# Local and global attention in front of a mixture of experts: the values as the stationary operand, in 64x64 parts, with the biases added on TensorE

## The chip, the cores and the metric

One core of a Trainium2 chip runs the kernel. The metric is the device time of one execution in microseconds. TensorE is called PE here (its weight loads have a row of their own, PEld), VectorE is DVE, ScalarE is ACT, GpSimd is POOL, and SyncE is SP, which issues most of the DMAs. Each of these engines takes its instructions in the order in which the program has them; they wait for each other through semaphores.

## The reference

Attention with a causal window of 96 keys and 8 global keys, with a bias that grows with the distance, in fp32; its output goes through a top-2 mixture of 8 experts.

```
q, k, v: [4, 8, 768, 64]
scores = q k^T / 8 + bias;  bias = -slope[h] * dist
keep   = (key < 8) | (0 <= query - key < 96)
a      = exp(scores - rowmax) / (rowsum + 1e-9)
x      = (a v), heads side by side: [3072, 512]
logits = x w_gate;  noisy = logits + log1p(exp(x w_noise)) * noise
out[token] = sum over the token's 2 best experts of weight * relu(x w1[e]) w2[e]
```

## The kernel before

Three stages follow each other: attention with the gate (tokens in 24 blocks of 128, six to a batch row), then the first expert, whose tokens are collected by gathers from a table in DRAM, then the other experts. The change touches the first stage and the gate, which is spread over it. In the expert stage only the order of the rows of w1 changes, on the host.

The unit of attention is `n`, one of 96: a block `g` of 128 queries and a pair index `u` of four. It covers two heads, which lie on the lower and the upper 64 partitions, for the two halves `s` of 64 queries. The first block of each batch row (i = 0) has 128 keys, every other block has 168 for each half (96 before, 8 global, 64 own). For each `n`:

- `product` (L485), issued for two `n` at a time: q in 64x64 parts is stationary and the keys are streamed, four parts of the array at once. The scores land in one bank of PSUM per `n`, out of a ring of three.
- `score` (L497, L501): for each half, one DVE instruction adds the bias, scales and takes the row's maximum, and one ACT instruction takes the exponential from SBUF.
- `trans` (L513, L515): PE transposes the probabilities, four parts of 128x128 for two halves and two ranges of keys, into a PSUM bank of the ring `at`, and one ACT copy of up to 512 columns brings them to SBUF.
- `attend` (L533): the transposed probabilities are the stationary operand, 128 columns each, and the values are streamed, 65 columns a head. The 65th column is all ones and gives the row's sum. DVE divides (L539 to L542) and has the block's output rows `xr`.

The gate of block `g` follows a few `n` later: `gate_t` transposes `xr` (L192) and ACT copies it (L194), `gate_l` multiplies by the gate's weights (L200) and ACT copies (L203), `gate_s` sums partial results (L206) and leaves the logits in a PSUM bank of their own. `gate_t` also issues the store of `xr` to DRAM. `route` is a generator that makes the top-2 choice and the table for a segment of blocks. Each call of `tick` takes one small step of it, nearly all on DVE.

The order is written out by hand: one loop over `n` calls `trans(n)`, `score(n+2)`, `attend(n-2)` and, for every other `n`, `product(n+3)`; a table `todo` puts loads, gates and the splitting of weights at chosen `n`. The PSUM rings matter below: `at` and `m` (transposes and the gate) share banks 3 and 4 in turn, so every tile taken from them waits until the tile before the last one has been read. At the end of the loop `turn` (L171) transposes the first expert's gathered tokens.

Of the kernel before, what the change touches and what calls it, by code (L numbers as in the profile page):

```python
# [20 lines left out]
P = 128  # L21
NP = 96
# [8 lines left out]
def tile_local_global_attention_then_moe(  # L31
# [3 lines left out]
    kT: bass.AP,  # L35
    v: bass.AP,
# [14 lines left out]
    D1 = D + 1  # L51
    E, _, F = w1.shape
    KC, FC = Dm // P, F // P
    NG = kT.shape[2] // NB - P
# [3 lines left out]
    WIN = NP + NG + Q  # L58
    windowed = 1 <= n_local <= NP + 1 and 0 <= n_global <= NG
# [16 lines left out]
    rings = {"sc": [0, 1, 2], "at": [3, 4], "m": [3, 4], "av": [5, 6], "lg": [7]}  # L76
    turns = {}
# [15 lines left out]
    sel = consts.tile([P, 2 * E], F32, name="sel")  # L93
# [89 lines left out]
    XR, XT, LS = {}, {}, {}  # L183
    lg = bank("lg")
    lgv = lg[:, :NT * 2 * E].rearrange("p (t e) -> p t e", t=NT)

    def gate_t(g):
        x = XR.pop(g).rearrange("p h d -> p (h d)")
        nc.sync.dma_start(xd[DUMP + g * P:DUMP + (g + 1) * P], x)
        ps = bank("m").rearrange("p (k t) -> p k t", k=KC)  # L190
        for k in range(KC):
            nc.tensor.transpose(ps[:, k], x[:, k * P:(k + 1) * P], ident)  # L192
        XT[g] = gp.tile([P, KC, P], F32, name="xt")
        nc.scalar.activation(XT[g], ps, AF.Copy)  # L194

    def gate_l(g):
        ps = bank("m")[:, :P]
        x = XT.pop(g)
        for k in range(KC):
            nc.tensor.matmul(ps[32 * k:32 * k + 32], wgn[:, k], x[:, k], start=True, stop=True,  # L200
                             tile_position=(0, 32 * k))
        LS[g] = gp.tile([P, P], F32, name="ls")
        nc.scalar.activation(LS[g], ps, AF.Copy)  # L203

    def gate_s(g):
        nc.tensor.matmul(lgv[:, g], LS.pop(g), sel, start=True, stop=True)  # L206
# [4 lines left out]
    def route(r):  # L211
# [4 lines left out]
        l = small.tile([P, SW, 2 * E], F32, name=f"l{r % 2}")[:, :w]  # L216
        u, t, p, ny, po = (small.tile([P, SW, E], F32, name=f"{x}{r % 2}")[:, :w] for x in ("u", "t", "p", "ny", "po"))
        n = l[:, :, E:]
        nc.vector.tensor_copy(l, lgv[:, a:z])
        yield  # L220
# [54 lines left out]
        ps = lg[:, NT * 2 * E:]  # L275
# [47 lines left out]
    with ExitStack() as actx:  # L323
# [6 lines left out]
        KB = NG + P  # L330

        def load_qk(b, j, i0):

            if i0 == 0:
                qs[b, j] = qbuf[j]
                ks[b, j] = aw.tile([P, KC, NP + NBH * KB], F32, name="ks")
            a = i0 * KB - (NP if j and not i0 else 0)
            c0 = j * NBH * KB
            nc.sync.dma_start(ks[b, j][:, :, NP + a:NP + (i0 + 1) * KB],
                              kT[b, :, c0 + a:c0 + (i0 + 1) * KB].rearrange("(k p) t -> p k t", p=P))  # L340
# [4 lines left out]
        HD = H * D1  # L345

        def load_v(g):

            b, i = divmod(g, NB)
            vs[g] = aw.tile([P, HD], F32, name="vs", bufs=4)  # L350
            nc.sync.dma_start(vs[g], v[b, i])
            if i:
                vp[g] = vpb[g % 4]
                nc.sync.dma_start(vp[g][:NP], v[b, i - 1, P - NP:])
                if i <= 4:
                    nc.sync.dma_start(vp[g][NP:], v[b, 0, :NG])

        if windowed:
            vpb = [ac.tile([NP + NG, HD], F32, name=f"vp{j}") for j in range(4)]
# [3 lines left out]
            load_qk(0, 0, 1)  # L363
            load_v(1)
            load_qk(0, 0, 2)
# [3 lines left out]
            bias0 = ac.tile([P, KC, 2, P], F32, name="bias0")  # L369
            bias = ac.tile([P, KC, 2, WIN], F32, name="bias")  # L370
            dist0 = ac.tile([Q, 2, P], F32, name="dist0")
            dist = ac.tile([Q, 2, WIN], F32, name="dist")
            far = 1e9 / min(slopes)

            def iota(d, base, step=0):

                nc.gpsimd.iota(d, pattern=[[step, d.shape[1]], [-1, d.shape[2]]], base=base, channel_multiplier=1,
                               allow_small_or_imprecise_dtypes=True)

            def reach(d, base, step, fill):  # L380

                n, w = d.shape[1:]
                if base < w:
                    nc.gpsimd.affine_select(out=d, in_=d, pattern=[[step, n], [-1, w]], compare_op=OP.is_ge,
                                            fill=fill, base=base, channel_multiplier=1)
                nc.gpsimd.affine_select(out=d, in_=d, pattern=[[-step, n], [1, w]], compare_op=OP.is_ge, fill=fill,
                                        base=n_local - 1 - base, channel_multiplier=-1)

            def biases(to, d, heads):
                for h in heads:  # L390
                    u, y = h // 4 * 2 + h % 2, h // 2 % 2
                    nc.vector.tensor_scalar(to[y * Q:(y + 1) * Q, u], d, -slopes[h] / scale, None, op0=OP.mult)
# [4 lines left out]
            iota(dist0, 0, Q)  # L397
            if n_global:
                reach(dist0[:, :, :n_global], 0, Q, float(n_local))
            reach(dist0[:, :, n_global:], -n_global, Q, far)  # L400
            make_identity(nc, ident)
            for x in range(2):
                c = NP - x * Q
                d = dist[:, x:x + 1]
                for a, z, base in (0, c, NP), (c + NG, WIN, x * Q):
                    iota(d[:, :, a:z], base)
                    reach(d[:, :, a:z], base, 0, far)
                nc.gpsimd.memset(d[:, :, c:c + NG], far)
                if n_global:
                    nc.gpsimd.memset(d[:, :, c:c + n_global], float(n_local))  # L410
            biases(bias0, dist0, range(H))

            AW = WIN + Q
# [503 lines left out]
```

## Time and profile before

| what | us |
|---|---|
| median of three executions (808.36 to 814.62) | 809.31 |
| the profiled execution | 814.3 |
| its span, first to last instruction | 812.6 |
| attention, first exponential to the first `turn` that waits | 6.5 to 184.0 |
| the gap and the slow clock behind it | 184.0 to 199.0 |
| the experts | 199.0 to 812.6 |

In the timeline, a row has its start, the time that the merged instructions cover, the engine, the line, the operation and how many it merges. In the table of groups, the two numbers behind the bar are the busy time in us and the mean duration in ns of one instruction. A matmul in fp32 has two records. Line numbers are those of the kernel before.

### The profile page before, as it was taken

Reading aid. Unit: us, or ns where it says so; the run is one execution under the profiler, and the core shown is the slowest. Engines: PE = TensorE matmul, PEld = TensorE weight load, DVE = VectorE, ACT = ScalarE, POOL = GpSimd, SP = SyncE. Lnnn points to the kernel's source line nnn. Section 1 sums busy time; section 2 is a strip of 40 time slices with the busy share of each in tenths; the row PEclk is TensorE's granted clock in tenths of the full one; section 3 lists DMA queues with packets and bytes.
Section 4 is the critical chain, followed back from the end, with each engine's and each line's share of the span. In section 5 each row is a group of like instructions: output and inputs, shape, how many; then the busy total and the mean of one; then the engine's idle time right before and its main releaser. Section 6 shows DMA issues by size and latency. Waiting matters only on the chain. (4 is left out here: it accounts for less than half of the span.)

```text
span 812.6 us, 14768 instructions
## 1 busy us (share of the span) xinstructions
PE 789.2 (97%) x5649; PEld 698.8 (86%) x5649; DVE 316.2 (39%) x1114; ACT 338.9 (42%) x736; POOL 223.6 (28%) x215
## 2 busy tenths in 40 slices
PE   7999999998999999999999999999999999999994
PEld 6988989987779989889898989898988989898983
DVE  6456565763803433234233413332342234233400
ACT  6778777773403433333233323333333334233311
POOL 2003330643835041222214031403132140302023
PEclk9999999997999999999999999999999999999997
DMA  8789595875275243434435253434453442432014
GB/s 263 251 275 304 177 212 192 171 195 188 54 145 119 90 108 112 92 95 125 87 90 123 75 110 101 109 106 84 105 131 78 99 111 87 102 74 31 1 25 63
DMA packets 64778, 100.77 MB, mean 124 GB/s; under 512 B 10666, under 2 KB 23210, under 8 KB 64698
## 3 DMA queue, kind: packets, MB, share of 16 engines
q1 hardware_dynamic: 49434, 73.05, 30.3%
q0 software_dynamic: 15264, 26.69, 18.3%
q8 instruction: 46, 0.75, 0.4%
q14 instruction: 34, 0.28, 0.1%
HBM read 71.46 MB, written 28.24 MB: 123 GB/s over the span
## 5 line engine op out<-in xcount | busy, mean ns | idle before, releaser
L730 POOL DMA_INDIRECT out_dram<-y,tba x28 | 44.6, 1592 | 257.6 <-ACT y L729 257.6
L745 PE MATMUL av<-w2h,hh 128*128 128x512 f32 x256 | 102.9, 402 | 0.0
L745 PE MATMUL av<-w2h,hl 128*128 128x512 f32 x256 | 101.4, 396 | 0.0
L745 PE MATMUL av<-w2l,hh 128*128 128x512 f32 x256 | 101.2, 395 | 0.0
L139 DVE TENSOR_TENSOR w1l<-raw,w1h 128x512 fp32r<-128x512 f32 x56 | 38.4, 690 | 148.2 <-ACT w1h L138 148.0
L712 PE MATMUL at<-xh,w1h 128*128 128x512 f32 (+1 forms) x256 | 90.0, 352 | 0.0
L712 PE MATMUL sc<-xh,w1h 128*128 128x512 f32 (+1 forms) x256 | 89.7, 350 | 0.0
L712 PE MATMUL at<-xl,w1h 128*128 128x512 f32 (+1 forms) x256 | 89.1, 348 | 0.0
L712 PE MATMUL at<-xh,w1l 128*128 128x512 f32 (+1 forms) x256 | 89.0, 348 | 0.0
L712 PE MATMUL sc<-xh,w1l 128*128 128x512 f32 (+1 forms) x256 | 88.7, 347 | 0.0
L712 PE MATMUL sc<-xl,w1h 128*128 128x512 f32 (+1 forms) x256 | 88.6, 346 | 0.0
L755 PE MATMUL av<-hh,w2h 128*128 128x300 f32 x256 | 79.0, 309 | 0.0
L730 POOL DMA_INDIRECT out_dram<-y,tbb x24 | 38.2, 1591 | 147.1 <-ACT y L729 146.8
L755 PE MATMUL av<-hl,w2h 128*128 128x300 f32 x256 | 77.0, 301 | 0.0
L755 PE MATMUL av<-hh,w2l 128*128 128x300 f32 x256 | 77.0, 301 | 0.0
L723 DVE SCALAR_TENSOR_TENSOR hl<-sc,hh 128x300 fp32r<-128x300 f32 (+1 forms) x62 | 35.8, 578 | 102.9 <-ACT hh L722 102.9
L501 ACT ACTIVATE a<-ns,mx 128x168 f32<-128x168 f32 (+1 forms) x192 | 71.5, 422 | 6.0 <-POOL a L417 4.2
L722 ACT ACTIVATE hh<-sc 128x300 fp32r<-128x300 f32 (+1 forms) x62 | 31.4, 507 | 100.0 <-PE sc L712 100.0
L533 PE MATMUL av<-vs,at 128*128 128x65 f32 x384 | 72.1, 277 | 0.0
L729 ACT ACTIVATE y<-av,tba 128x512 f32<-128x512 f32 x28 | 19.2, 688 | 125.9 <-issue 106.2
L722 ACT ACTIVATE hh<-at 128x300 fp32r<-128x300 f32 (+1 forms) x62 | 31.4, 507 | 85.4 <-PE at L712 85.4
L304 POOL DMA_INDIRECT tbl<-ent,sli x48 | 48.1, 1002 | 65.4 <-DVE mx L497 41.4
(142 smaller groups left out, 1658.0 us busy)
## 6 DMA issues: line engine op xcount, KB each, us to landing
raw<-in_w SPq DMA_DIRECT2D x32, 1024.0 KB
out_dram<-zero SPq DMA_DIRECT2D x14, 512.0 KB
vs<-in_v SPq DMA_DIRECT2D x24, 260.0 KB
qbuf<-in_q SPq DMA_DIRECT2D x24, 256.0 KB
xd<-xr SPq DMA_DIRECT2D x24, 256.0 KB
ks<-in_k SPq DMA_DIRECT2D x20, 272.0 KB
vp<-in_v SPq DMA_DIRECT2D x20, 195.0 KB
ks<-in_k SPq DMA_DIRECT2D x4, 464.0 KB
```

Of the source, the lines that this page charges most:

```text
L139: eng.tensor_sub(lo, t, hi.bitcast(F32))
L304: ins = nc.gpsimd.indirect_dma_start(out=tbl, out_offset=bass.IndirectOffsetOnAxis(ap=sli[:, i, j:j + 1], axis=0), in_=ent[:, i, j], in_of ...
L501: nc.scalar.activation(A[n][:, s, c:c + w], ns[:, s, :w], AF.Exp, bias=mx[:, s:s + 1], scale=-1.0)
L533: nc.tensor.matmul(ps[:, h % 4], a[:kk, y * w + c0:y * w + c0 + P], t[:kk, c], start=kk < P or not i, stop=kk == P)
L712: nc.tensor.matmul(ps, w[:, k, fs], x[c][:, k], start=n == 0, stop=n == 3 * KC - 1)
L722: nc.scalar.activation(hh[c][:, f], ps, AF.Relu)
L723: nc.vector.scalar_tensor_tensor(hl[c][:, f], ps, 0.0, hh[c][:, f].bitcast(F32), op0=OP.max, op1=OP.subtract)
L729: nc.scalar.activation(y, ps, AF.Copy, scale=r[:, 1:2].bitcast(F32))
L730: ins = nc.gpsimd.indirect_dma_start(out=out, out_offset=bass.IndirectOffsetOnAxis(ap=r[:, 0:1], axis=0), in_=y, in_offset=None, bounds_ch ...
L745: nc.tensor.matmul(ps, x[0][:, f, cols], w[:, f], start=n == 0, stop=n == 3 * FC - 1)
L755: nc.tensor.matmul(ps, w[:, f, cols], x[1][:, f], start=n == 0, stop=n == 3 * FC - 1)
```

## The change

It rewrites attention and the gate. The unit of the loop is now a step `s` of two `n` (48 steps).

- The 168 keys lie in three parts of 64 columns (two full parts, and one with 32 local and 8 global keys, padded). `product` streams 128 and then 40 columns in 64x64 parts and adds the bias with one bf16 matmul for each part of the array, stationary a 64x64 identity, streamed a precomputed bias of 384 columns. q is scaled beforehand (`scale_q`: ACT for the first three blocks, POOL for the rest).
- `score` takes the maximum of both halves with one DVE instruction, and the exponentials read PSUM directly, over 192 columns, with a sum from ACT's accumulator. Four banks hold scores.
- `trans` transposes both `n` of a step together: six transposes of 128x128, and two ACT copies of 384 columns.
- `attend` has the values stationary in 64x64 parts and streams the probabilities, 128 or 64 columns, for both `n`; the result is transposed (head dimension on the partitions) and accumulates in two fixed banks.
- `heads_out` copies a block's result to SBUF by two DVE instructions. `gate_l` reads it as it is, `gate_x` transposes it back and DVE divides, and `gate_s` transposes the products, which DVE divides and sums over the heads. `sums` prepares the reciprocals with five DVE instructions.

```
-                        nc.tensor.matmul(SC[n + x][y * Q:(y + 1) * Q, s], qs[b, j][r, 2 * i0 + s, u + y],
-                                         ks[b, j][r, u + y, k0:k0 + w], start=True, stop=True,
+                            nc.tensor.matmul(SC[n + x][y * Q:(y + 1) * Q, s, c:c + wc],
+                                             qs[b, j][r, 2 * i0 + s, u + y], m, start=s == 0 and full, stop=False,
...
+                    nc.tensor.matmul(SC[n + x][y * Q:(y + 1) * Q], identb[r], (bias if i else bias0)[r, u // 2, y],
+                                     start=False, stop=True, tile_position=(x * D, y * Q), skip_group_check=True)
...
-                nc.vector.tensor_tensor_reduce(
-                    out=ns[:, s, :w], in0=ps[:, s], in1=bias[:, u, s] if i else bias0[:, u, s],
-                    scale=-scale, scalar=3e38, op0=OP.add, op1=OP.min, accum_out=mx[:, s:s + 1])
-                c = s * Q if i else AW - P
-                nc.scalar.activation(A[n][:, s, c:c + w], ns[:, s, :w], AF.Exp, bias=mx[:, s:s + 1], scale=-1.0)
-                tick()
+            nc.vector.tensor_reduce(mx, ps[:, :, :min(w, P + NS)], op=OP.max, axis=AX.X, negate=True)
+            for s in range(2):
+                nc.scalar.activation(A[n][:, s, :w // Q, n % 2], ps[:, s].rearrange("p (c t) -> p c t", t=Q), AF.Exp,
+                                     bias=mx[:, s:s + 1], accum_out=SUM[g][:, u, s:s + 1])
+            tick()
...
+        def trans(n, s):
...
+            ps = bank("at")[:, :m * P].rearrange("p (c t) -> p c t", t=P)
+            for c in range(m):
+                nc.tensor.transpose(ps[:, c], A[n][:, s, c].rearrange("p x t -> p (x t)"), ident)
...
+            nc.scalar.activation(AT[n][:, s, :m], ps, AF.Copy)
...
+                        nc.tensor.matmul(to if s is None else to[:, s], t[r, h * D:(h + 1) * D],
+                                         a[r, :, c, o] if s is None else a[r, s, c, o], start=j == 0,
...
+    def gate_x(g):
+        ps = bank("m")
+        for u in range(HP):
+            nc.tensor.transpose(ps[:, u * P:(u + 1) * P], OT[g][:, u], ident)
...
+    def gate_s(g):
+        ps = bank("m")[:, :P]
+        nc.tensor.transpose(ps, LS.pop(g), ident)
...
+                at(n + 2, sums, g)
+                    at(n + 3, gate_x, g)
+                    at(n + 4, gate_s, g)
...
+            for s in range(NPR + 1):
+                n = 2 * s
...
+                    product(n + 2)
+                    score(n + 2)
+                if s:
+                    attend(n - 2)
+                if s > 2 and s % 2:
+                    gate_l(s // 2 - 1)
...
+                    score(n + 3)
+                if s and s % 2 == 0:
+                    heads_out(s // 2 - 1)
...
+                    trans(n, 0)
+                    tick()
+                    trans(n, 1)
...
+                for f, a in todo.pop(s, []):
+                    f(*a)
```

The loads change with it: the earlier values come in up to six DMAs a block instead of two, and the keys of half a batch row in two DMAs at once instead of three in turn.

What stands on PE around a product, before. Names are those of the program: `a` the probabilities, `at` the transposed ones, `av` the attention output, `sc` the scores; the brackets name the engines that the instruction waits for.

```order
L513 MATMUL at<-ident,a_182 128x2x64 [waits Activation_49]
L513 MATMUL at<-ident,a_182 128x2x64 x3
L533 MATMUL av<-vp_102,at 128x65
L533 MATMUL av<-vs,at 128x65
L533 MATMUL av<-vp_102,at 128x65
L533 MATMUL av<-vs,at 128x65
L485 MATMUL sc<-ks,qbuf_107 64x168
L485 MATMUL sc<-ks,qbuf_107 64x168 [waits DVE_49]
L485 MATMUL sc<-ks,qbuf_107 64x168 x6
L200 MATMUL m<-xt,wgn 32x128 [waits Activation_49]
```

The same place after, in an odd step: `gate_l` (L205), the six transposes of `trans` (L554), `gate_x` (L196), and then the next step's product (L524) into the fixed banks.

```order
L205 MATMUL m<-ot,wgn 32x128 [waits PE_49]
L205 MATMUL m<-ot,wgn 32x128 x3
L554 MATMUL at<-ident,a_229 128x128 [waits DVE_49]
L554 MATMUL at<-ident,a_229 128x128 x2
L554 MATMUL at<-ident,a_229 128x128 [waits Activation_49]
L554 MATMUL at<-ident,a_229 128x128 x2
L196 MATMUL m<-ident,ot 128x128 [waits Activation_49]
L196 MATMUL m<-ident,ot 128x128 x3
L524 MATMUL fixed_76<-ks,qbuf_111 64x128
L524 MATMUL fixed_79<-ks,qbuf_111 64x128
```

Behind `trans` there now stands a gate instruction that takes the ring's next bank and waits for ACT; the product of the next step is behind it. In an even step the same place is held by the one transpose of `gate_s`.

On ACT, before: each `n` has its two exponentials and then the copy of another `n`.

```order
L515 ACTIVATE at<-at 128x512 [waits PE_49,Activation_49]
L501 ACTIVATE a_181<-ns,mx 128x168 [waits DVE_49]
L501 ACTIVATE a_181<-ns,mx 128x168 [waits DVE_49,Activation_49]
L515 ACTIVATE at<-at 128x512 [waits PE_49,Activation_49]
L501 ACTIVATE a_182<-ns,mx 128x168 [waits DVE_49]
L501 ACTIVATE a_182<-ns,mx 128x168 [waits DVE_49,Activation_49]
L515 ACTIVATE at<-at 128x512 [waits PE_49,Activation_49]
```

And after, one odd step: four exponentials with `gate_l`'s copy among them (L208), and then both copies.

```order
L543 ACTIVATE a_228,sum<-fixed_74,mx 128x3x64 [waits DVE_49]
L543 ACTIVATE a_228,sum<-fixed_74,mx 128x3x64 [waits Activation_49]
L208 ACTIVATE ls<-m 128x128 [waits PE_49,Activation_49]
L543 ACTIVATE a_228,sum<-fixed_75,mx 128x3x64 [waits DVE_49]
L543 ACTIVATE a_228,sum<-fixed_75,mx 128x3x64 [waits Activation_49]
L557 ACTIVATE at<-at 128x384 [waits PE_49,Activation_49]
L557 ACTIVATE at<-at 128x384 [waits PE_49]
```

The copies of a step have moved behind all four exponentials of the next one.

More of the change, by code (lines that the diff above doesn't have):

```diff
@@ L21 @@
 P = 128
-NP = 96
+NL = 32
 TA = 4
@@ L425, in gate_consts @@
             nc.vector.memset(wgn, 0.0)
[L426 to L429 removed]
+            for y in range(2):
+                nc.sync.dma_start(wgn[y * Q:(y + 1) * Q, :, y * 2 * E:(y + 1) * 2 * E],
+                                  w_gn.rearrange("(k y p) e -> y p k e", y=2, p=D)[y])
         def route_consts():
@@ L519, in attend @@
         def attend(n):
             g, u, b, i = geo(n)
-            w = 2 * P if i else P
             a = AT.pop(n)
-            if u % 2 == 0:
-                pav[g, u // 2] = bank("av")[:, :4 * D1].rearrange("p (h d) -> p h d", h=4)
-            ps = pav[g, u // 2]
-            blocks = [(vs[g], P, w - P)]
+            steps = [(vs[g][:, 0], 0, None), (vs[g][:, 1], 1, None)]
             if i:
-                blocks.insert(0, (vp[g], NP + NG, 0))
-            for y in range(2):
-                h = u // 2 * 4 + 2 * y + u % 2
-                c = slice(h * D1, (h + 1) * D1)
-                for t, kk, c0 in blocks:
-                    nc.tensor.matmul(ps[:, h % 4], a[:kk, y * w + c0:y * w + c0 + P], t[:kk, c],
-                                     start=kk < P or not i, stop=kk == P)
@@ new lines, in heads_out, with sums @@
+        def heads_out(g):
+            OT[g] = gp.tile([P, HP, P], F32, name="ot", bufs=2)
+            c = slice(g % 2 * 2 * P, (g % 2 + 1) * 2 * P)
+            for x, t in enumerate((ota, otb)):
+                nc.vector.tensor_copy(OT[g].rearrange("p (j x) t -> p x j t", x=2)[:, x],
+                                      t[:, c].rearrange("p (j t) -> p j t", t=P))
+        def sums(g):
+            t = SUM.pop(g)
+            d = aw.tile([P, HP, 2], F32, name="den", bufs=2)
+            RD[g] = gp.tile([P, H], F32, name="rd", bufs=3)
+            for s in range(2):
+                for y in range(2):
+                    nc.vector.tensor_scalar(d[s * Q:(s + 1) * Q, :, y], t[y * Q:(y + 1) * Q, :, s], 1e-9, None,
+                                            op0=OP.add)
+            nc.vector.reciprocal(RD[g], d.rearrange("p u y -> p (u y)"))
@@ L778, in tile_local_global_attention_then_moe @@
                 zero_out(NZ + f)
-            up(0, 0, f, f < 4, {4: gate_t, 8: gate_l, 11: gate_s} if f == 0 and windowed else {})
+            up(0, 0, f, f < 4, {3: gate_x, 6: gate_l, 9: gate_s} if f == 0 and windowed else {})
             if f < 2:
```

353 lines of the change are left out of this document (188 added, 165 removed).

## The prediction

> **What bounds the kernel now.** I read the busy time of the engines by stretches first, then the timeline of PE inside attention, then the waits. The stretches (window, its length, busy time and count of PE, PEld, DVE, ACT, POOL, granted clock, DMA share, GB/s):
>
> ```profile
> 20.00:180.00 160.00, 159.96 (x1983) 143.04 (x1982) 96.63 (x636) 121.69 (x310) 45.66 (x49) 1.00 0.82 226
> 184.00:187.20 3.20, 0.14 (x3) 0.01 (x1) 0.20 (x2) 0.88 (x2) 2.59 (x3) 1.00 0.83 266
> 187.20:199.00 11.80, 11.80 (x74) 10.76 (x75) 5.33 (x19) 2.86 (x6) 0.93 (x2) 0.57 0.33 115
> ```
>
> Only attention changes, and PE bounds it: 159.96 of 160 us, with 143.04 us of weight loads, while ACT has 121.69 and DVE 96.63. At its end there are 3.2 us without PE, and then 11.8 us at a clock of 0.57. The timeline of PE, from two places:
>
> ```profile
> 46.08 0.67 PE L485 MATMUL sc<-ks,qbuf 64*64 64x128 f32 x16
> 91.58 0.67 PE L485 MATMUL sc<-ks,qbuf 64*64 64x128 f32 x16
> ...
> 63.09 0.80 PE L485 MATMUL sc<-ks,qbuf 64*64 64x168 f32 x16
> 63.83 0.43 PE L200 MATMUL m<-xt,wgn 128*32 128x128 f32 x8
> 64.18 0.66 PE L513 MATMUL at<-ident,a 128*128 128x128 f32 x4
> 64.84 0.39 PE L533 MATMUL av<-vs,at 128*128 128x65 f32 x2
> 65.07 0.39 PE L533 MATMUL av<-vp,at 104*128 104x65 f32 x2
> 65.29 0.39 PE L533 MATMUL av<-vs,at 128*128 128x65 f32 x2
> 67.11 0.80 PE L485 MATMUL sc<-ks,qbuf 64*64 64x168 f32 x16
> ```
>
> A product is issued every two `n`: at 63.09 and 67.11, 4.02 us apart. From the first product of one batch row (46.08) to that of the next (91.58) it is 45.5 us for 12 of them. `attend` issues two matmuls in 0.225 us, 0.112 each, though 65 streamed columns are half of the 128 loaded: its weight loads set its pace. ACT waits for PE, and not the other way round:
>
> ```profile
> ACT at L515 <- PE at L513: 24.1, 50, 0.9
> ```
>
> **The change part by part.** The prices, by group in attention (20 to 180 us), with two bursts' durations from the line of the product:
>
> ```profile
> L501 ACT ACTIVATE a<-ns,mx 128x168 f32<-128x168 f32 x144 | 54.5, 428 | 1.7 <-DVE mx L497 1.5
> L501 ACT ACTIVATE a<-ns,mx 128x128 f32<-128x128 f32 x24 | 8.2, 394 | 0.0
> L515 ACT ACTIVATE at<-at 128x512 f32<-128x512 f32 x73 | 43.4, 594 | 21.0 <-PE at L513 20.5 <-issue 0.3
> L515 ACT ACTIVATE at<-at 128x256 f32<-128x256 f32 x12 | 4.6, 382 | 3.8 <-PE at L513 3.6
> L203 ACT ACTIVATE ls<-m 128x128 f32<-128x128 f32 x21 | 5.8, 277 | 10.8 <-PE m L200 10.4
> L497 DVE CUSTOM_DVE_ANT_0 ns<-sc,bias 128x168 f32<-128x168 f32 x144 | 41.3, 325 | 0.5 <-ACT a L501 0.3
> L497 DVE CUSTOM_DVE_ANT_0 ns<-sc,bias 128x128 f32<-128x128 f32 x24 | 5.7, 285 | 0.0
> L497 DVE DVE_READ_ACCUMULATOR2_ANT mx<- 128x1 f32 x168 | 13.9, 83 | 0.0
> L485 PE MATMUL sc<-ks,qbuf x672: 268/303/355, 22.4 to 178.4; 64*64 64x168 f32 x144, 64*64 64x128 f32 x24
> ```
>
> *PE's own work falls.* The 16 product matmuls run in four rounds of four. First to last start takes 0.80-0.30 = 0.50 us with 168 columns and 0.67-0.27 = 0.40 with 128, so a round is 0.143 or 0.109 us after a start of 0.05. The new `attend` has two rounds of 128 columns and eight of 64; a 64-column load is half of 0.112, 0.056, so 0.22+0.45 = 0.67 us a step, where before two `n` took 16 x 0.112 = 1.79. Transposes go from eight to six at 0.109, 0.65 for 0.87. The product gets 0.44 (four rounds of 128) and 0.22 (four of 40, no less than their load), and a bias round of 384 columns in one pass: 0.16, by half of fp32's 0.85 ns a column. The gate costs 0.43 + 0.39 in odd steps and 0.11 in even ones; a change of the array's shape about 0.2, twice a step. That is 2.2 to 3.3 us, 2.95 on the mean.
>
> *But PE now waits in each step.* By the order of the instructions, the gate's transposes (`gate_x` in odd steps, `gate_s` in even ones) stand behind `trans` and take the ring's next bank but one: the bank that this step's first ACT copy has to empty. That copy stands on ACT behind the four exponentials of the next step; those wait for DVE's maxima, those for the product; and the product after it stands on PE behind the waiting gate. So product, maximum, exponentials, copy and gate become one chain with nothing overlapped. The hand-overs are short:
>
> ```profile
> 62.78 0.39 PE L533 MATMUL av<-vs,at 128*128 128x65 f32 x2
> 63.20 0.16 DVE L539 TENSOR_SCALAR den<-av 128x4 f32<-128x4 f32 x1 [0.69 <-PE av L533]
> ...
> 67.08 0.75 ACT L501 ACTIVATE a<-ns,mx 128x168 f32<-128x168 f32 x2
> ...
> 63.82 0.16 PEld L200 LDWEIGHTS m<-xt,wgn 128*32 128x32 f32 x8 [0.24 <-ACT at L515]
> 64.18 0.42 PEld L513 LDWEIGHTS at<-ident,a 128*128 128x128 f32 x4 [0.20 <-ACT a L501]
> 64.57 0.19 PEld L533 LDWEIGHTS av<-vp,at 104*128 104x128 f32 x1
> ```
>
> PE to DVE is 63.17 to 63.20, 0.03 us. Two exponentials take 0.75, so the second starts 0.75-0.43 = 0.32 after the first. Shape changes leave PEld idle 0.20 to 0.24. The chain for a step of a block with i > 0:
>
> 1. product, first start to last result: 0.05+0.44+0.22+0.16 and 0.16 of depth (0.303 less 0.143 streamed): 1.03.
> 2. hand-over and one maximum of 336 columns: DVE goes at (325-285)/40 = 1.0 ns a column, so 0.325+0.168 = 0.49; with both hand-overs 0.55.
> 3. four exponentials of 192 columns: ACT goes at 0.85 ns a column, so 0.32+0.02 each: 1.38.
> 4. copy of 384 columns, halfway from 0.382 to 0.594: 0.49; hand-over 0.03.
> 5. the gate to the next product: one transpose, of which 0.06 lies ahead of the change of shape, or four, 64.18 to 64.57, 0.39; and 0.2 for the shape.
>
> An even step is 1.03+0.55+1.38+0.52+0.26 = 3.74. An odd one has 0.33 more for `gate_x` and 0.28 for `gate_l`'s copy among the exponentials (0.277 less 0.1 of overlap, and 0.1 until PE has it): 4.35. Mean 4.05. PE's other work in the step (`attend`, `gate_l`, `trans`, some 1.9 us with a change of shape) lies beside items 2 and 3, which are as long; DVE's copies of `heads_out` and the division behind `gate_x` lie beside the product and the exponentials. If the wait for the copy went, PE's 2.95 would be next.
>
> The gate's idle of 0.24 us in the row of L200 above is already a wait of this kind, and cheap, since ACT's copies come early in the cycle there. The Trainium skill, Perfetto Trace Analysis, Matmuls under Optimizing Tensor Performance, wants independent matmul groups rotated through different PSUM banks, so that the emptying of one overlaps the next group's matmuls. The two banks shared by `trans` and the gate don't do that here; with banks enough for it the sum would be that of the first rival below.
>
> Two terms have no row. The sums from ACT's accumulator need reading out; DVE's reading is a row of 0.083 us, an ACT instruction with hardly any columns at most 0.277-0.1 = 0.18 plus a gap. I take the former: 4 x 0.083 = 0.33 a step, ends 0 and 0.8. A gain is excluded, since no exponential is dropped. And DVE is late for the maximum in every other step: behind `gate_s` it has a multiply and a reduction over 128 columns (0.285 each by the row of 128), five small instructions of `sums` (0.16 each by the row of `den`), 1.4 us in all, and up to two steps of `route`; the next product's result comes 0.26+1.03 = 1.3 us after. Mean 0.2 a step, ends 0 and 0.4. That gives 4.58. A step with i = 0 saves 0.27 (product), 0.08, 0.21 and 0.11: 3.91. A batch row is 10 x 4.58 + 2 x 3.91 = 53.6 us against 45.5.
>
> *Ends of the stage.* The chain is whole from step 3 to step 46: 43 steps at a mean of (53.6/12) 4.47 are 192 us. The three steps ahead of it cost some 8 us from the first exponential (ACT's four exponentials with their reads, 1.7, and two copies, 0.8, each), the last one 4 until `turn` (items 1 to 3, the reads and six transposes): 204.5, against 184.0-6.5 = 177.5 before. So +27.
>
> ```profile
> 6.53 1.28 ACT L501 ACTIVATE a<-ns,mx 128x128 f32<-128x128 f32 x4 [4.22 <-POOL a L417]
> ...
> 1.31 0.49 SPq L342 DMA_DIRECT2D qbuf<-in_q  x1
> ...
> 9.83 0.35 SPq L342 DMA_DIRECT2D qbuf<-in_q  x1
> 10.22 0.43 SPq L351 DMA_DIRECT2D vs<-in_v  x1
> ...
> 4.76 1.51 PE L485 MATMUL sc<-ks,qbuf 64*64 64x128 f32 x18 [4.76 <-DMA qbuf<-in_q]
> ...
> PEld sc L171 <- DMA xg<-xd,tb: 3.3, 1, 3.3
> ```
>
> The start gets later. ACT now scales three blocks of q ahead of the first exponential, and the third of them is the 15th DMA. Before, the 15th was issued at 10.22, held back by earlier landings, and the first q took from 1.31 to at most 4.76 to be used. So ACT goes on at about 12 to 13 us instead of 6.53: +6, ends +3 and +7. POOL's longer list of masks ends earlier than that. The other new DMAs (68 more small ones for the earlier values) have slack: a block's loads are issued three blocks ahead, 27 us.
>
> The end gains. `turn` waited 3.3 us for gathers, and the slow clock behind it cost about 11.8 x 0.43 = 5.1. The table's last steps are paced by `tick` and POOL, and slower steps bring `turn` later than the gathers: -6, ends 0 and -8. The expert stage has the same instructions.
>
> Sum: +27+6-6 = +27 on the span of 812.6, so 840 for a profiled execution with 1.7 us around it (814.3). That execution was 5 us over the median of 809.31; the median should be 836.
>
> **The rivals.** *PE stays the bound (faster).* If the copy came in time, a step would be PE's 2.95 (2.2 for i = 0), and four batch rows save 4 x (45.5-33.9) = 46 us: 809-46+6 = 769. For it: weight loads do set `attend`'s pace, and they are halved. Against it: the wait on ACT stands in the order, and ACT alone has 4 x 0.34 + 2 x 0.4 us to do between two gates. Chance 0.07. The Trainium skill, TensorEngine Tiling (Array Packing), When to Use Tiling, recommends just this swap with column tiling where the streamed side has at most 64 columns. Its PSUM Bottleneck section warns that tiling speeds up TensorE but not the emptying of PSUM; the chain above is a case of that.
>
> *The chain is there, but its unknown terms are nothing (no change).* Without the accumulator's reading and the late maximum a step is 4.05, and 43 steps take 23 us less: 813. Chance 0.14; DVE's reads of its accumulator lie right under the next instruction, which speaks for it, DVE's queue against it.
>
> *The accumulator empties ACT's pipeline (slower yet).* Each exponential then costs its full 0.45 and a read of 0.18 instead of 0.34+0.08: +0.2 x 4 x 43, +35, 871. Nothing in the trace shows such a wait. Chance 0.06.
>
> *The clock drops.* After 3.2 us of idle PE the granted clock was 0.57. PE now idles in each step, but for 1 to 2 us at a time. At 0.57 PE's share of the chain, 1.4 us a step, grows by 1.1: +47, 883. Chance 0.04. The Trainium skill, TensorE: Matmul & The Clock Gate, tells in its section on psum-queue depth-cycling of short idles between groups of matmuls that make the clock swing; in this trace, gaps of 0.2 us left it at 1.00.
>
> **How the numbers follow.** The chain as priced has 0.69, at 836. With the unknown terms at their ends it runs from 813 (rival two) to 836 + 0.67 x 43 = 865. A range of 812 to 867 leaves out the fast rival, most of the two slow ones and a little at the lower end: no more than 2 in 10. About 1% (8 us) is what a measurement of this kernel can tell from no change. Faster by that: 0.08, rival one and a little more. Within it, 801 to 817: 0.15, rival two and the lowest end of the forecast. Slower: 0.77.
>
> **What would show it.** Right: PE's busy share in attention falls well under 90%, with idle ahead of the gate's transposes (L196, L212) put down to ACT's copy (L557), and ACT idle ahead of exponentials put down to DVE's maximum; products 3.7 to 5 us apart. A row of its own for the accumulator gives the term of 0.083. First exponential near 12 us; no wait at `turn`. Wrong: products 3 us apart, PE without gaps, or the time lost in other places than attention.

## The result, and the profile after

The changed kernel takes 872.4 us (median of 4, 869.5 to 875.5) where the kernel before takes 809.2: a ratio of 1.0763, 95% interval 1.071 to 1.0815, or 63 us more. The forecast was 836, 27 us more, with a range of 812 to 867. A second comparison gave 873.3 against 812.4, ratio 1.0724 (1.0673 to 1.0776). The profiled execution took 871.39 us with a span of 869.1. In the first and the fourth of the five sets of experiments below, the kernel before itself took 852.7 and 860.0 us instead of 809 to 812, so from these two sets only quiet steps and single rows are read.

The first exponential starts at 11.67, where it was 6.53:

```profile
11.67 0.35 ACT L543 ACTIVATE a<-fixed,mx 128x128 f32<-128x128 f32 x1
```

A step is called quiet when nothing of the route and no work on GpSimd delays it. The chain stands in the profile as forecast. First the stretch from the product of step 4 to that of step 46 (window, length, busy time of PE, PEld, DVE, ACT, POOL, granted clock, DMA share, GB/s):

```profile
28.00:237.00 209.00, 149.03 (x3559) 117.71 (x3555) 121.36 (x457) 110.90 (x456) 74.95 (x69) 0.92 0.60 172
```

PE is busy for 149.03 of 209 us, 71%, where it had 159.96 of 160; and no other engine has more. Two steps of PE, and the ACT that it waits for in the first:

```profile
41.55 0.88 PE L524 MATMUL fixed<-ks,qbuf 64*64 64x128 f32 x32
...
44.75 0.55 PE L554 MATMUL at<-ident,a 128*128 128x128 f32 x3 [0.64 <-ACT ls L208]
45.93 0.66 PE L196 MATMUL m<-ident,ot 128*128 128x128 f32 x4 [0.64 <-ACT at L557]
46.52 0.88 PE L524 MATMUL fixed<-ks,qbuf 64*64 64x128 f32 x32
...
48.18 0.87 PE L554 MATMUL at<-ident,a 128*128 128x128 f32 x6
50.36 0.33 PE L212 MATMUL m<-ident,ls 128*128 128x128 f32 x1 [1.31 <-ACT at L557]
50.62 0.68 PE L524 MATMUL fixed<-ks,qbuf 64*64 64x128 f32 x20
```

```profile
43.61 0.42 ACT L543 ACTIVATE a<-fixed,mx 128x192 f32<-128x192 f32 x1 [2.00 <-DVE mx L541]
43.93 0.19 ACT L543 ACTIVATION_READ_ACCUMULATOR a<-fixed,mx 128x1 f32 x1
44.02 0.41 ACT L543 ACTIVATE a<-fixed,mx 128x192 f32<-128x192 f32 x1
...
44.42 0.27 ACT L208 ACTIVATE ls<-m 128x128 f32<-128x128 f32 x1
...
45.37 0.89 ACT L557 ACTIVATE at<-at 128x384 f32<-128x384 f32 x2
```

The odd step takes 4.97 us from product to product (41.55 to 46.52), the even one 4.10 (46.52 to 50.62). Both gates, L196 and L212, wait for ACT's copy at L557 while the next product stands behind them, and ACT waits 2.00 us for the maximum. The exponentials and their readings over the whole stretch, by group:

```profile
L543 ACT ACTIVATE a<-fixed,mx 128x192 f32<-128x192 f32 (+1 forms) x168 | 67.7, 414 | 93.9 <-DVE mx L541 84.0 <-DVE sli L308 3.4 <-DVE m L258 2.4
...
L543 ACT ACTIVATION_READ_ACCUMULATOR a<-fixed,mx 128x1 f32 x168 | 34.3, 204 | 0.0
```

ACT is idle for 93.9 us ahead of its exponentials; before, it was 1.7. The waits of the whole stretch (total, times, longest) say the same, and name a third that the prediction lacks, the second group of `trans` behind the copy of `gate_l`. The last two rows belong to the route and are read further below:

```profile
ACT a L543 <- DVE mx L541: 84.0, 40, 3.2
...
PE m L212 <- ACT at L557: 21.4, 19, 1.6
PE at L554 <- ACT ls L208: 19.7, 18, 2.3
...
PE m L196 <- ACT at L557: 14.0, 21, 1.3
...
DVE mx L541 <- PE fixed L292: 2.6, 2, 1.6
...
PE fixed L288 <- ACT a L543: 1.3, 1, 1.3
```

Where the time went, by the forecast's own pieces (us of the profiled executions; the forecast's pieces add up to 839, which it has as 840):

| piece | forecast | measured | from |
|---|---|---|---|
| to the first exponential | 12.5 | 11.67 | row of ACT |
| to the product of step 3 | 8 | 8.57 | product at 20.24 |
| 43 steps, 3 to 45 | 192 | 216.0 | product of step 46 at 236.24 |
| from there to `turn` | 4 | 7.28 | `turn` at 243.52 |
| `turn` to the end | 622.6 | 625.6 | span 869.1 |

So 24 of the 30 us that the forecast lacks lie in the chain. I took its 42 steps from 27.57 to 236.24 apart by the starts of product, maximum, exponentials, copies and next product, with the usual value of each kind of step as its quiet one. Quiet, they are 18 x 4.97 + 18 x 4.10 + 3 x 4.67 + 3 x 3.43 = 187.6 us, 4.47 a step: the forecast's mean. The 21.1 us on top are, to within 0.2:

| excess over quiet steps | us |
|---|---|
| first maximum late (VectorE), and its hand-over | 8.0 |
| second maximum late (VectorE), third exponential behind it | 2.1 |
| the route's counts on PE, in a score bank | 3.3 |
| product, bias and gate slow (clock) | 6.9 |
| a pause of PE without a wait | 1.0 |

The 43rd step is step 3, 7.33 us long: PE waits there for the gate's weights. SP could issue their load only after VectorE had cleared their tile, behind a step's maxima and `heads_out` (PE, VectorE, then SP):

```profile
24.53 0.42 PE L205 MATMUL m<-ot,wgn 128*32 128x128 f32 x8 [2.41 <-DMA wgn<-in_w_gn]
```

```profile
20.28 0.17 DVE L454 MEMSET wgn<- 128x128 f32 x1
```

```profile
20.48 1.39 SPq L456 DMA_DIRECT2D wgn<-in_w_gn  x2
```

VectorE's lateness has three sources. In every quiet odd step the five `sums` instructions stand ahead of the maximum. A step of the route ahead of the second maximum can itself wait for ACT, as in step 37, where it held VectorE for 1 us:

```profile
191.04 0.18 DVE L233 TENSOR_SCALAR t<-u 128x40 f32<-128x40 f32 x1 [1.00 <-ACT u L231]
```

In the steps in which GpSimd works, one of the `sums` instructions takes much longer (VectorE, then GpSimd):

```profile
87.71 0.29 DVE L214 TENSOR_TENSOR lh<-m,rd 128x128 f32<-128x128 f32 x1 [1.06 <-PE m L212]
88.04 0.38 DVE L216 TENSOR_REDUCE LG<-lh 128x16 f32<-128x128 f32 x1
88.33 1.78 DVE L595 TENSOR_SCALAR den<-sum 64x4 f32<-64x4 f32 x4
...
90.33 0.50 DVE L541 TENSOR_REDUCE mx<-fixed 128x2 f32<-128x336 f32 x1
```

```profile
87.21 2.51 POOL L143 TENSOR_TENSOR w1l<-raw,w1h 128x512 fp32r<-128x512 f32 x2
```

The product of this step starts at 87.65, so its maximum could start at 88.7; it starts at 90.33. The four additions take 1.78 us, where four take 0.69 in a quiet step; their mean over the chain is 238 ns for four columns:

```profile
L595 DVE TENSOR_SCALAR den<-sum 64x4 f32<-64x4 f32 x84 | 20.0, 238 | 0.8
```

The route's counts are small matmuls (L288 to L292). Before the change they had the bank of the logits; now they use spare columns of a score bank. In steps 22 and 34 the second maximum, which reads that bank, waited for them, and in step 40 they waited for ACT's exponentials and the transposes of `trans` stood behind them. The three steps lost 3.3 us. In step 45 PE paused for 2.17 us, with no wait for another engine, ahead of `gate_l`, whose copy ACT has ahead of the third exponential:

```profile
232.85 0.34 PE L576 MATMUL fixed<-at,vp 64*64 64x64 f32 x8 [2.17 <-issue]
```

Eight of the 42 products are slow, for example that of step 34, with 1.52 us for what takes 0.88 at 41.55. With the bias, its last result comes 1.84 us after its start, and in a quiet step 1.04:

```profile
173.12 1.52 PE L524 MATMUL fixed<-ks,qbuf 64*64 64x128 f32 x32
...
174.42 0.54 PE L530 MATMUL fixed<-bias,identb 64*64 64x384 bf16 x4
```

At the end `turn` waits for nothing any more, as forecast:

```profile
243.52 1.04 PE L175 MATMUL sc<-ident,xg 128*128 128x128 f32 x8
```

### The profile page after: what moved, and what is told of

Read it like the earlier page. It is cut to its first block, busy times and chain, and to the rows that moved or that the text cites. A ratio compares the mean times of both kernels' runs of the same rounds, so it can differ in the third digit from the quotient of the medians.

```text
span 869.1 us, 18240 instructions
## 1 busy us (share of the span) xinstructions
PE 776.4 (89%) x7401; PEld 668.9 (77%) x7401; DVE 347.3 (40%) x920; ACT 329.1 (38%) x907; POOL 255.7 (29%) x241
## 5 line engine op out<-in xcount | busy, mean ns | idle before, releaser
L543 ACT ACTIVATE a<-fixed,mx 128x192 f32<-128x192 f32 (+1 forms) x192 | 77.1, 413 | 99.3 <-DVE mx L541 86.2
L554 PE MATMUL at<-ident,a 128*128 128x128 f32 x272 | 48.7, 306 | 23.9 <-ACT ls L208 19.7
L797 DVE SCALAR_TENSOR_TENSOR hl<-at,hh 128x300 fp32r<-128x300 f32 (+1 forms) x62 | 35.8, 578 | 67.6 <-ACT hh L796 67.6
```

Of the source, the lines that this page charges most:

```text
L543: nc.scalar.activation(A[n][:, s, :w // Q, n % 2], ps[:, s].rearrange("p (c t) -> p c t", t=Q), AF.Exp, bias=mx[:, s:s + 1], accum_out=SUM ...
L554: nc.tensor.transpose(ps[:, c], A[n][:, s, c].rearrange("p x t -> p (x t)"), ident)
L797: nc.vector.scalar_tensor_tensor(hl[c][:, f], ps, 0.0, hh[c][:, f].bitcast(F32), op0=OP.max, op1=OP.subtract)
```

## The experiments

Eighteen runs were made, in five sets, each set beside the kernel before; two are of the kernels themselves, and three repeat a run of the fourth set.

**The gate behind the next product.** The chain's cause, taken away:

```
-                    at(n + 3, gate_x, g)
-                    at(n + 4, gate_s, g)
+                    for k, f in (4, gate_x), (5, gate_s):
+                        if n + k < NPR:
+                            late.setdefault(n + k, []).append((f, g))
...
                     score(n + 3)
+                for f, g in late.pop(s, []):
+                    f(g)
```

> The gate's transposes (x and the logits) are issued one step later on TensorE: behind the next product, behind attend and both maxima, instead of ahead of the next product; the logits' staging tile gets a second buffer; everything else is as in the changed kernel. Theory (the bank wait ties product, maximum, exponentials, copy and gate into one serial chain): the next product no longer waits for ACT's copy, a step falls from 4.1 to 5.0 us in quiet places to TensorE's own 2.95 or a little over, 3.0 to 3.4, so 43 steps take 55 to 80 us less: 792 to 817. Rival (the steps are long because of what TensorE has to execute, its lower clock and its many small loads): TensorE's busy time stays, the time stays above 855.

Measured: 881.6 in the first set, ratio 1.0312. Quiet steps fell from 4.97 and 4.10 to 3.62 and 3.57, so the chain is broken, but not to the 3.0 to 3.4 expected. The time is above the rival's 855, but in this set it decides nothing: the changed kernel did not run there.

**The sums behind both maxima**, and the same additions **as reductions** in their old place:

```
-                at(n + 2, sums, g)
...
                     score(n + 3)
+                if s > 2 and s % 2:
+                    sums(s // 2 - 1)
```

```
-                    nc.vector.tensor_scalar(d[...], t[...], 1e-9, None, op0=OP.add)
+                    nc.vector.tensor_reduce(d[...], t[...], op=OP.add, axis=AX.X)
```

> Only the five small VectorE instructions that prepare the division (sums) move: from the end of an even step, ahead of the next product's maxima on VectorE, to behind both maxima. Theory (VectorE comes late to the maximum because of them, by 0.4 us in a quiet odd step and by 1.2 to 1.9 in those in which GpSimd works): first maxima come back to 1.1 us after the product's start, 14 to 19 us less: 853 to 858. Rival (the odd steps are longer because of the logits' copy on ACT and the route, or the clock): within 4 us of 872.

> The four additions of 1e-9 to the sums (VectorE tensor_scalar over 4 columns; a sum is at least 1, where fp32 doesn't see 1e-9) are written as four reductions over one element each, in the same place: same count, same order. Theory (a tensor_scalar from SBUF to SBUF is held until a running GpSimd instruction ends, and this makes VectorE late in the steps with the weight splits): no such instruction is longer than 0.25 us, the steps at 77, 88, 98 and 109 us lose about 1.2 us each, the others with the q scaling 0.1: 4 to 8 us less, 864 to 868. Rival (they are slow for their own shape or for reading other partitions): the reductions are as slow, 872 within 3 us.

Measured in the first set: 887.7 and 892.0, ratios 1.0374 and 1.044. Behind the maxima, quiet odd steps fall from 4.97 to 4.60; what that is worth in time this set can't tell. As reductions the additions take 149 ns each whatever GpSimd does (they leave out the 1e-9), and the steps that took 6.44, 6.19, 6.16 and 7.15 take 5.43, 5.47, 5.36 and 5.54: 4.1 us in four steps.

```profile
L595 DVE TENSOR_REDUCE den<-sum 64x4 f32<-64x4 f32 x80 | 12.0, 149 | 0.8
```

**The accumulator's readings.**

```
-                                     bias=mx[:, s:s + 1], accum_out=SUM[g][:, u, s:s + 1])
+                                     bias=mx[:, s:s + 1])
```

> The exponentials don't sum: no reading of ACT's accumulator; the sums are set to 1 once a block on GpSimd, so the output isn't normalised. Theory (in the chain an exponential with its reading takes 0.40 us where it took 0.34 without): 0.06 to 0.09 x 4 a step, 43 steps, 10 to 15 us less than the changed kernel's 872: 857 to 862. Rival A (the reading empties ACT's pipeline): 30 us or more less, under 843. Rival B (the readings lie beside other work): 872 as it is, within 3 us.

> The changed kernel without the accumulator's readings: each head's sums are replaced by a constant, the mean sum of that head (2.6 to 47), so the output is normalised only roughly, and the experts get about as many tokens as before. Theory (a reading adds 0.09 us to each exponential of the chain, as quiet steps of the run without sums showed: 4.60 and 3.73 instead of 4.97 and 4.10): 42 steps at 0.37 less, 13 to 17 us less than the changed kernel, ratio 1.055 to 1.062. Rival (what the readings free is taken by VectorE's lateness, which stays): under 7 us, ratio above 1.065.

> The same kernel as in the earlier run with the heads' mean sums in place of the accumulator's readings (so the output is normalised only roughly), where the kernel before took 860. Where it takes 809 to 813: Theory (0.37 us a step): ratio 1.055 to 1.062. Rival (VectorE's lateness takes what is freed): above 1.065.

With sums of 1 the experts' loads changed (974.3), so that only the quiet steps count: 4.60 and 3.73, 0.37 less each. With the mean sums, in the fourth set, the quiet steps are the same (883.0, ratio 1.0247). In the fifth: 851.9 against 809.8, ratio 1.051 (1.0491 to 1.0529), some 17 to 20 us less than the changed kernel. The 42 steps took 192.3 instead of 208.7. The readings cost what the theory says, a little more than its range.

**The kernels beside each other.**

> The changed kernel as it is, beside the kernel before, on the chip of these runs, where the kernel before took 852.7 in the earlier runs instead of 809.2. If the change costs what it cost in the recorded comparison, it takes 63 us more than the kernel before, ratio 1.06 to 1.08. If the long steps with TensorE's clumped matmuls (0.7 us apart in the steps at 139 to 155, 187, 203 and 231 us of the experiments' traces) come on top of the change alone, the ratio is above 1.08; if the kernel before has them too, it is under 1.06.

> The kernel before as it is, with a profile from the chip of these runs. Theory (TensorE gets its instructions slowly at times on this chip, in clumps 0.7 us apart, whatever the kernel): attention shows gaps in bursts of the same line's matmuls, 30 to 40 us in sum, and the experts' stage is as long as in the recorded profile (617). Rival (the expert stage is longer on this chip, or DMA): attention is 189 us long as recorded, and the difference lies behind it.

Measured: ratio 1.0724, and 812.9 for the kernel before, whose attention showed no gap inside a line's burst. The change costs the same again, and clumps are at most a small part of it: the changed kernel's stretch had two gaps of this kind, 1.9 us in all. The kernel before took its usual time in this set, so whether clumps can lengthen it too was not put to the test.

**Gate and sums behind; the gate in its own places.** In the second of these x is transposed right behind the product, and the logits go to unused columns of a score bank:

```
+                    for f, g in late.get(s, []):
+                        if f is gate_x:
+                            gate_t(g)
...
-        ps = bank("m")[:, :P]
+        ps = scb[2][:, 2 * WIN:] if col else bank("m")[:, :P]
```

> Both moves at once: the gate's transposes behind the next product (as in the earlier run with that alone, 881.6 on a chip where the kernel before took 852.7), and the sums behind both maxima. Theory (with the chain broken VectorE's lateness is hidden in most steps, but not in those in which GpSimd works): quiet steps as with the gate alone, 3.6 us, the steps with weight splits 1 to 2 us shorter, 4 to 8 us less than the gate alone. Rival (VectorE is no longer on the path at all): within 3 us of the gate alone.

> As the run with both moves, and the gate spread so that no transposes of the probabilities wait for it: x is transposed right behind the product with its division behind the maxima, and the logits go into columns of a score bank that no score uses. Theory (what is left of the step, 3.6 us against TensorE's 2.95, is the wait of the transposes for the two shared banks): quiet steps of 3.0 to 3.2 us, attention 18 to 25 us shorter than with both moves, faster than the kernel before by 5 to 25 us where TensorE gets its instructions in time. Rival (3.6 us is what VectorE and ACT need, or TensorE's rate of instructions): within 5 us of the run with both moves.

Measured: 845.7, ratio 1.0428 (1.0381 to 1.0475), and 838.1, ratio 1.031 (1.0265 to 1.0355), against 873.3 for the changed kernel in the same set. The wait of the chain and the `sums` ahead of the maxima are thus worth 27.6 us together, and the rest of the sharing 7.6 more. The second kernel was expected to beat the kernel before by 5 to 25 us; it takes 26 more. What the `sums` add to the gate alone can't be read, since the gate alone ran in the first set. Two steps of the first of them on PE:

```profile
36.59 0.88 PE L524 MATMUL fixed<-ks,qbuf 64*64 64x128 f32 x32
...
39.41 0.87 PE L554 MATMUL at<-ident,a 128*128 128x128 f32 x6 [0.48 <-ACT ls L208]
40.22 0.88 PE L524 MATMUL fixed<-ks,qbuf 64*64 64x128 f32 x32
...
43.31 0.55 PE L554 MATMUL at<-ident,a 128*128 128x128 f32 x3 [0.46 <-DVE xr L198]
43.79 0.88 PE L524 MATMUL fixed<-ks,qbuf 64*64 64x128 f32 x32
```

The steps are 3.63 and 3.57 long, and now `trans` waits for the gate's readers, in the same two banks. With the gate in its own places the quiet steps are 3.21 and 3.52: near the 3.0 to 3.2 expected in the even ones, longer in the odd ones.

**VectorE on time; another start; filled waits.** For the first, all of a step's `tick` calls stand behind both maxima, with the sums as reductions there too. For the second, ACT scales one block of q ahead of the first exponential instead of three, and `gate_consts` goes from step 2 to step 0. For the third:

```
                     trans(n, 1)
+                    if more_to_do:
+                        for _ in range(8):
+                            nc.tensor.transpose(scb[n % 4][:, :P], ident, ident)
```

> The changed kernel with its chain as it is, and everything that makes VectorE late for a maximum moved behind both maxima of a step: the sums (as reductions, which didn't wait for GpSimd in the earlier run) and all eight route steps. Theory (of the 42 steps' 208.7 us, 187.4 are the quiet chain and some 15 are VectorE's lateness on top, with 0.4 us more in every odd step): first maxima 1.1 us after the product's start everywhere, 15 to 23 us less than the changed kernel's 63 us over the kernel before, ratio 1.05 to 1.06. Rival (ACT or the gate takes the place of VectorE at once): under 5 us.

> The changed kernel with another start: ACT scales only q's first block ahead of the first exponential, the second behind it, the third a step later, and the gate's weights are loaded two steps earlier. Theory (the start costs 5 us until the first exponential, and some 8 in the first four steps, of which the wait for the gate's weights is 2.4): first exponential at 8 us instead of 11.7, the step that waited for the weights 2 us shorter, 4 to 7 us less than the changed kernel. Rival (what is won at the start is lost again at the end, waiting for the route): under 2 us.

> The changed kernel with eight transposes of the identity (0.87 us, their result unused) behind each step's transposes, where TensorE would wait for ACT's copy. Theory (the lower granted clock comes from TensorE's idle time, and costs 5 to 7 us: products of 1.84 instead of 1.04 us in eight steps): the granted clock in attention rises from 0.90 to 0.97 or more, products are 1.04 us everywhere, 4 to 7 us less than the changed kernel. Rival A (the clock falls for another reason): the same slow products, 0 to 5 us more. Rival B (the wait is not idle time but the chain runs over TensorE's own work): 0.87 us a step more, +35 us.

Measured: 853.7, ratio 1.0548 (1.0501 to 1.0596); 866.2, ratio 1.0674 (1.0634 to 1.0714); 872.9, ratio 1.0764 (1.0729 to 1.0799). With VectorE on time the 42 steps took 191.6 instead of 208.7 us, and the time was 14 to 17 us less than the changed kernel's two ratios give. The other start gave 4 to 7 us by the same reckoning, as expected: the product of step 5 came at 26.08 instead of 32.47, though at `turn` only 2.3 of these 6.4 us were left (241.2 instead of 243.5), and the experts' part was 2.5 shorter. The filled waits raised the clock from 0.92 to 0.97 and left 3 slow products of 8, yet gained nothing: where a wait lay ahead of the filler, the filler itself ran slowly and held up the gate behind it, as here, where eight transposes took 1.91 us instead of 1.04:

```profile
87.17 0.79 PE L554 MATMUL at<-ident,a 128*128 128x128 f32 x3 [2.07 <-ACT ls L208]
87.75 1.91 PE L752 MATMUL fixed<-ident 128*128 128x128 f32 x8
```

So idle PE does go with the lower clock here, but what the clock costs in net was not settled.

**Do the terms add?** Start and VectorE together, the chain left alone:

> The changed kernel with its chain, with the other start and with VectorE on time, both as in the runs that had one of them (ratio 1.067 and 1.055). Theory (they are separate terms of the miss): the gains add, 17 to 18 us and 6 to 7 us, ratio 1.043 to 1.050, 845 to 851 where the kernel before takes 810; what is left then is the chain as it was forecast (836) with the clock's part. Rival (the time won at the start is lost again behind VectorE or at the end): ratio 1.052 to 1.058.

> The same kernel as in the earlier run with the other start and VectorE on time, where the kernel before took 860. Where it takes 809 to 813: Theory (the gains add): ratio 1.043 to 1.050. Rival (one hides the other): 1.052 to 1.058.

Measured: 885.8 in the fourth set (1.0284, with clumps), 847.4 in the fifth: ratio 1.0463 (1.0434 to 1.0492). They add. What remains is 11 us over the forecast.

**Everything, and a faster route.**

> The gate in its own places, the sums as reductions behind the maxima, the route's steps behind both maxima, and the other start, all in one. Theory (each cause was an addition to the path): quiet steps of 3.2 and 3.5 us as with the gate in its own places, the steps with weight splits 3 us shorter each, the start 4 us shorter: 12 to 20 us less than the gate in its own places alone (ratio 1.031), ratio 1.005 to 1.017. Rival (TensorE then runs short of instructions, or turn waits for the gathers): ratio 1.02 to 1.03.

> All together (ratio 1.021), with twelve instead of eight route steps behind the maxima of a step. Theory (the gain of the broken chain is held back at the end by the route: PE waits 3.5 us for the gathers, and the clock is low behind that): gathers 4 to 8 us earlier, no wait of TensorE for them, 3 to 8 us less, ratio 1.011 to 1.018. Rival A (GpSimd's scatters set the pace of the route, 1.28 us each): the same wait, within 2 us. Rival B (more route steps make VectorE late for the maxima, which costs more): 1.022 to 1.03.

> The same kernel as in the earlier run with everything together and twelve route steps, where the kernel before took 860. Where it takes 809 to 813: Theory (the gathers held back the gain): ratio 1.011 to 1.018. Rival A (GpSimd's scatters set the pace): 1.019 to 1.022. Rival B (VectorE late): above 1.022.

Measured: 827.0, ratio 1.0211 (1.0153 to 1.027); with twelve route steps 864.6 in the fourth set (1.0052) and 827.1 in the fifth, ratio 1.0209 (1.0173 to 1.0245). The first is the rival's ratio, and the last is in the range of the rival with GpSimd's scatters, but for another reason than it gives. No version beat the kernel before. In the first of them attention's last product came at 181.28, but PE then waited for the gathers, and the experts began at 202.0 (194.3 in the kernel before's profile of the second set):

```profile
192.19 0.66 PE L175 MATMUL sc<-ident,xg 128*128 128x128 f32 x4 [2.76 <-DMA xg<-xd,tb]
```

The faster route took that wait away and put another in its place. On GpSimd the load of the table, which waits for the scatters to land, now comes ahead of the last scaling of q, which the change had put there; PE's product waits for it (GpSimd, then PE):

```profile
183.86 0.60 POOL L329 DMA_DIRECT2D tb<-tbl  x1 [5.81 <-DMA tbl<-ent,sli]
184.49 1.53 POOL L366 TENSOR_SCALAR qbuf<-qbuf 128x512 f32<-128x512 f32 x1
```

```profile
186.08 1.52 PE L530 MATMUL fixed<-ks,qbuf 64*64 64x128 f32 x32 [6.62 <-POOL qbuf L366]
```

None of the three theories had this wait, so the last ratio speaks for none of them.

## Why the prediction was wrong in size, point by point

- **The chain** was right: 4.07 and 5.08 forecast for quiet even and odd steps (with the reading and the late maximum), 4.10 and 4.97 measured, and with the gate behind the product 3.57 and 3.62. The rival in which PE stays the bound falls with it. The 0.2 us for a change of shape is not shown by its rows: they put these gaps down to ACT, and the text itself also reads the 0.24 at L200 as a wait for ACT. The Trainium skill's advice to rotate independent groups of matmuls through different PSUM banks (Perfetto Trace Analysis, Matmuls under Optimizing Tensor Performance) is what the gate in its own places follows in part; the runs agree with it, by the 7.6 us that this alone gave.
- **The readings** were nearly right: 0.33 us a step forecast, 0.37 measured in quiet steps. The rival in which a reading empties ACT's pipeline falls: exponentials lie 0.41 us apart with a reading, not 0.63.
- **VectorE late for the maximum** is the step that failed most: 0.2 us a step, ends 0 and 0.4. The quiet steps have that (0.38 in odd ones, half of it on the mean), but the term was priced from quiet rows alone. By the rows 10.1 us more lie in steps with route work or with GpSimd at work, which makes 0.45 a step. With VectorE on time the 42 steps took 17.1 us less, 0.41 a step, of which some 3 us are slow products that became fewer. So this term is at most a third of the 30 us. That `sums` and GpSimd's work could get into each other's way was nowhere in the list of what the change adds.
- **Terms put at nothing.** The upper end of 867 moved the two unknown terms alone, so the smaller misses had no room: the clock (6.9 us), the route's counts in a score bank (3.3), PE's pause (1.0), the gate's weights (2.4), and the two misses at the end (3.3 and 3.0). With VectorE's part alone the time would have been inside the range.
- **The first steps**: 20.5 forecast for the product of step 3, 20.24 measured. Behind it PE waited 2.41 us for the gate's weights, whose load stands behind VectorE's clearing of their tile.
- **The clock** was a rival at 0.57 and 47 us. It came, but at 0.92, with 6.9 us in slow products and gates: a term of the sum, not a case of its own.
- **The end**: the wait at `turn` went, 3.2 us. The other 2.8 us of the forecast gain did not come: `turn` to the end is 625.6, and was 625.4 from the first transposes of `turn`. The last stretch ahead of `turn`, forecast at 4, took 7.28: the forecast stops at one step's transposes, but another step's `attend`, `gate_l` and transposes follow them, and the product was slow.
- **Against the median**: the forecast took off 5 us because the execution profiled before lay that far above its median. The one profiled after lies 1 below its own. So 30 us of span became 36 of time. This part is chance.

## What to carry to other kernels

Price a serial chain from its quiet steps, but then go through the loaded ones: each small instruction ahead of a waited-for one on the same queue costs what it takes at its worst place, not at its usual one. When work moves to a shared engine (here q's scaling to GpSimd), look both for what it blocks beside itself and for what later stands ahead of it in that queue. Let the range carry every term that stands at nothing, the clock and the shared banks too. Taking away the wait that binds helps only as far as the next wait: with gate and sums behind, `turn` came 36 us earlier than in the changed kernel of the same set (209.2, 245.3) and the end 31, and the shared banks, the gathers and GpSimd's queue were next.

## What the runs showed of the hardware

**A VectorE addition waits for GpSimd.** At 88.52 one addition over four columns took 1.225 us; it ended at 89.75, and GpSimd's subtraction that had begun ahead of it ended at 89.72. Over the chain, additions without GpSimd beside them take 162 ns on the mean and at most 168, beside a weight split up to 1236. Reductions of the same size took 149 throughout. The Trainium skill, SBUF — State Buffer, section Who interferes with whom, has a rule that fits this: a `tensor_scalar` in its fast mode and a GpSimd instruction exclude each other on a shared pair of ports for a whole instruction, and a `tensor_reduce` on this chip never contends. That the additions ran in that mode no row shows.

**PE pauses with no wait for another engine.** In the first and the fourth set PE's short matmuls came in clumps 0.7 us apart, with no wait for another engine; one such spell is that of the gate behind the product:

```profile
183.82 0.35 PE L576 MATMUL fixed<-at,vp 64*64 64x64 f32 x1 [0.48 <-issue]
184.54 0.26 PE L576 MATMUL fixed<-at,vp 64*64 64x64 f32 x1 [0.37 <-issue]
185.26 0.35 PE L576 MATMUL fixed<-at,vp 64*64 64x64 f32 x1 [0.46 <-issue]
```

In the second set it appears as single gaps inside a burst of one line, in the kernel with the gate in its own places 9.0 us in four of them; the changed kernel had one of 2.2 us in its recorded profile, the kernel before none:

```profile
141.56 0.58 PE L212 MATMUL fixed<-ot,wgn 128*32 128x128 f32 x2 [3.34 <-issue]
```

That the supply of instructions is short there is inferred; no run tested it. The traces' records of DMA packets speak for it in the single gaps: by the count of its packets, a DMA queue of the kind instruction, q8, brings PE's instructions (60 packets of 16 KB for 14802 records of PE and PEld), and of the 14 gaps over 1 us in the recorded profile and in the second, third and fifth set, 10 end 1.1 to 1.5 us after the end of such a packet (138.56 to 140.15 for the gap that ends at 141.56). The clumps show no such link; their cause stays open; the kernel before has no trace in their sets. The Trainium skill, Runtime: NRT & Kernel Launch, section Instruction fetch mechanics, says that an engine's queue is refilled in blocks of 256 instructions and that this is mostly hidden; if the inference holds, these gaps show a stretch where it was not. The changed kernel's attention issues 17.0 matmuls per us of its stretch (3559 in 209), the kernel before's 12.4 (1983 in 160), and the kernel with gate and sums behind 20.6 (3481 in 169).
